# Step 0's bonus as a second run of scores with a second mask, seven weight buffers, step 0's outputs issued from ScalarE's queue, and k's multiplication in other slots

## The chip, the cores and the metric

The kernel runs on one core of a Trainium2 chip. The metric is device time in microseconds (us), a median of runs. TensorE (PE) multiplies matrices, VectorE (DVE), ScalarE (ACT) and GpSimd (POOL) work on tiles, SyncE (SP) issues most of the transfers (DMAs).

## The reference

A recurrent attention over 768 tokens, 4 batches and 8 heads of 48 columns feeds two dense layers:

```python
for t in range(S):
    cur = einsum('bhd,bhe->bhde', u * kt, vt)            # the bonus of the token itself
    y[:, :, t] = einsum('bhd,bhde->bhe', rt, state + cur)
    state = w[..., None] * state + einsum('bhd,bhe->bhde', kt, vt)
x = (sigmoid(x @ w_gate) * (x @ w_val)) @ moe_w_out      # 384 -> 1536 -> 384
out = square(max(x @ w_in, 0)) @ moe2_w_out              # 384 -> 2048 -> 384
```

## The kernel before, in words

**Attention.** The tokens are cut into 6 steps of 128, and a step of one batch is a unit: unit n is step n // 4, batch n % 4. A unit has four inputs: kT and rT (k and r by columns), kv (v and k by rows) and rn (r by rows); lines 98 to 108 load them in the order kv, rn, kT, rT. `attn_prep` (L235) multiplies kT and rT by powers of w on DVE. `attn_scores` (L282) forms all products of r and k on PE. The bonus, r·(u·k) of the same token, is made apart: `attn_pre` (L228) multiplies rn by k and by u on POOL, `attn_sum` (L243) adds up on DVE, and `attn_diag` (L251) puts the eight sums on the antidiagonal of `am` with eight ACT instructions. `attn_mask` (L323) copies the scores under the mask into `am` on DVE. `attn_kh` (L259) multiplies the k rows by `th` on POOL (called kh below), and `attn_sums` (L304) forms the unit's state sums from them on PE. `attn_out` (L340) multiplies `am` with v, reads the state, calls the next unit's scores and sums, copies the sums (`us`) and the output (`ys`) out on ACT, and sends `ys` to `xr` with two DMAs, and four more after a step's last unit (L386 to L392).

**Dense layers.** A tile is 128 columns of a hidden layer for 512 tokens. In the first layer it takes 9 matmuls `pg`, 9 matmuls `pv` and, one tile later, 9 matmuls into `two` and `po`. ACT makes the sigmoid of `pg`, DVE multiplies it with `pv` into `s`, ACT casts it to `gh`, and POOL (in step 0's phase) or DVE makes the rest `gl`.

**Weights.** They come as 64-bit words. `convert` (L124) takes one piece further at each call: ACT and DVE work on the raw piece n (L156, L158), DVE joins piece n-1 (L148, `wt_`), ACT casts piece n-2 (L135) and POOL makes its rest (L136, `wu`). Tile f of the first layer needs pieces 3f (pg), 3f+1 (pv) and 3f+2 (out). `load_raw` keeps NRB = 4 raw buffers.

**Order.** It is written out by hand and each engine runs its list in order. Step 0's four units are done first, alone, with matmuls on an idle tile between them (`warm`). Then phase 0 does tiles 0 to 6 of step 0 while the four units of step 1 are put into its slots by `unit_ops` (L474), eight operations each, kh last of all, just ahead of the next unit's `attn_out`. Phase 1 does step 1's 12 tiles with step 2's units in the slots, and so on. Tiles 7 to 11 of step 0 come after step 5.

**Completion counters.** The program gives its DMAs eight counters in turn, and a DMA is issued only when the one before it on the same counter has landed.

Of the kernel before, what the change touches and what calls it, by code (L numbers as in the profile page):

```python
# [7 lines left out]
F32 = mybir.dt.float32  # L8
# [12 lines left out]
L = 64  # L21
# [21 lines left out]
def tile_kernel(  # L43
# [31 lines left out]
    w_sb = cp.tile([DP, HP], F32, name="w_sb")  # L75
    u_bc = cp.tile([C, H * D], F32, name="u_bc")
# [10 lines left out]
    first = [  # L87
        [wp.tile([P, m], F32, tag="w", name="first", bufs=NW) for _, m, _ in PIECES]
        for _ in range(IN_W)
    ]  # L90
# [73 lines left out]
    def tables():  # L164
# [9 lines left out]
        q = lambda j: px[:, :, j : j + 1].to_broadcast([DP, HP, R])  # L174
        p0 = sp.tile([DP, HP, R], F32, tag="am", name="p0", bufs=2)
        nc.gpsimd.memset(d1, 0.0)
# [91 lines left out]
    def mm64(bank, q, out, lhsT, rhs):  # L270
# [11 lines left out]
    def attn_scores(n):  # L282

        if n >= NU:
            return
        k, r = k_t[n], r_t[n]
        banks, pa_t[n] = (1, 2), pas
        if n < B:

            two = pp.tile([P, 2, T], F32, tag="o", name="pa0")  # L290
            banks, pa_t[n] = (3, 4), two[:, :, 0 : HP * L].rearrange("p r (j t) -> p r j t", j=HP)
            opened.difference_update([(m, q) for m in banks for q in range(2)])
        pa = pa_t[n]
# [46 lines left out]
    def attn_out(n):  # L340
# [18 lines left out]
        if n + 1 < B:  # L359
            attn_scores(n + 1)  # L360
        for j in range(HP):
# [23 lines left out]
        x = xraw[c]  # L385
        nc.sync.dma_start(out=x[0:48, :, b], in_=ys[0:48, b, 0:KT])  # L386
        nc.sync.dma_start(out=x[48:96, :, b], in_=ys[64:112, b, 0:KT])
        if b == B - 1:
            nc.sync.dma_start(out=x[96:128, 0], in_=ys[0:32, :, KT])
            nc.sync.dma_start(out=x[96:112, 1], in_=ys[32:48, :, KT])  # L390
            nc.sync.dma_start(out=x[112:128, 1], in_=ys[64:80, :, KT])
            nc.sync.dma_start(out=x[96:128, 2], in_=ys[80:112, :, KT])  # L392

# [80 lines left out]
    def unit_ops(c, tiles):  # L474
# [4 lines left out]
        if c == 1:  # L479
            slots[0].append(lambda: (attn_pre(B + 1), attn_prep(B + 1)))  # L480
            slots[1].append(lambda: (attn_kh(B + 1), attn_sum(B + 1)))
            slots[2].append(lambda: (attn_diag(B + 1, 0), attn_diag(B + 1, 1)))
        for b in range(B):
# [129 lines left out]
    with tc.manual_schedule():  # L613
# [25 lines left out]
        attn_scores(0)
        attn_sum(0)  # L640
        attn_diag(0, 0)
        attn_diag(0, 1)
# [3 lines left out]
        attn_mask(0)
        attn_sum(1)
        attn_diag(1, 0)
        attn_sums(0)
        attn_us(0)  # L650
        attn_diag(1, 1)
        for n in range(B):
            m = n + 2
            if m < B:
                attn_pre(m)
                attn_kh(m)
                attn_prep(m)
            warm(WARM_OUT[n])
            attn_out(n)
            if m <= B:  # L660
                attn_mask(n + 1)
            if m < B:
                attn_sum(m)
                attn_diag(m, 0)
                attn_diag(m, 1)
# [120 lines left out]
```

## Time and profile before

| what | us |
|---|---|
| median of 3 runs (lowest to highest) | 977.85 (976.94 to 978.19) |
| the profiled execution, its own time | 979.93 |
| its span in the trace | 978.1 |
| PE busy | 947.2 (97%) |
| DVE, ACT, POOL busy | 450.8, 402.9, 132.4 |

The page's map of 40 slices is full for PE from about the sixth slice on; only the first 120 us or so hold slices in which PE is under 9 tenths and the granted clock under full speed. So the rows of this document are taken from there. The profiled execution lies 2.08 us above the median of the runs.

### The profile page before, as it was taken

How to read it: one execution, taken by the hardware profiler on the slowest of the kernel's cores; microseconds unless marked ns; L12 is line 12 of the kernel's file. 1: busy time of each engine (PE TensorE's matmuls, PEld its weight loads, DVE VectorE, ACT ScalarE, POOL GpSimd, SP SyncE). 2: the span in 40 equal slices, each digit the busy share in tenths (PEclk: the TensorE clock that was granted, in tenths of full speed). 3: DMA queues.
4: the chain of work that ended last, by engine and by line, in shares of the span. 5: the costliest groups of instructions: out<-in, count | busy, mean ns of one | idle time of the engine just before them, and what ended most of it. 6: DMA issues, size and time to landing. Idle time of an engine off the chain costs nothing.

```text
span 978.1 us, 16626 instructions
## 1 busy us (share of the span) xinstructions
PE 947.2 (97%) x6898; PEld 757.1 (77%) x6898; DVE 450.8 (46%) x742; ACT 402.9 (41%) x826; POOL 132.4 (14%) x121
## 2 busy tenths in 40 slices
PE   7788899999999999999999999999999999999997
PEld 4466678888888888887888888888888888888886
DVE  5677756754344345423344364433433433434332
ACT  3765565533333323322466463332422322323322
POOL 7455544200000000000133121000000000000000
PEclk7987999999999999999999999999999999999999
DMA  8674545532122222001244540010100100100000
GB/s 305 179 254 140 157 151 153 172 92 64 53 61 85 66 87 88 18 8 44 90 125 127 162 130 1 1 64 1 38 28 1 65 0 1 65 1 1 32 1 33
DMA packets 42235, 76.86 MB, mean 79 GB/s; under 512 B 5168, under 2 KB 17584, under 8 KB 42160
## 3 DMA queue, kind: packets, MB, share of 16 engines
q1 hardware_dynamic: 42160, 75.80, 24.5%
q8 instruction: 54, 0.88, 0.4%
q14 instruction: 21, 0.17, 0.1%
HBM read 60.05 MB, written 11.01 MB: 73 GB/s over the span
## 4 chain that ended last, share of the span: by engine, by line
PE 89%; DVE 2%; DMA 2%; POOL 2%; ACT 1%; SPq 1%; issue 1%; DVEq 0%; POOLq 0%; ACTq 0%
PE pg L445 35%; PE two L464 16%; PE pv L445 15%; PE po L464 12%; PE att L464 7%; PE att L272 4%; DMA first<-in_rkv 2%; SPq L104 1%; DMA xr<-ys 0%; POOL wu L136 0%; POOL gl L428 0%; ACT am L257 0%; ACT raw L156 0%; PE pw L611 0%; POOL first L264 0%
## 5 line engine op out<-in xcount | busy, mean ns | idle before, releaser
L445 PE MATMUL pg<-xh,wu 128*128 128x512 f32 x1008 | 318.3, 400 | 6.5 <-ACT wu L135 3.1
L445 PEld LDWEIGHTS pg<-xh,wu 128*128 128x128 f32 x1008 | 191.0, 190 | 55.6 <-ACT wu L135 3.6
L445 PE MATMUL pg<-xl,wu 128*128 128x512 f32 x504 | 196.7, 398 | 0.3 <-DVE xl L428 0.2
L597 ACT CAST gh<-s 128x512 fp32r<-128x512 f32 (+1 forms) x169 | 104.7, 620 | 192.5 <-DVE s L593 119.0
L596 DVE TENSOR_TENSOR s<-s 128x512 f32<-128x512 f32 (+1 forms) x97 | 66.6, 687 | 181.5 <-ACT s L595 181.5
L428 DVE TENSOR_TENSOR gl<-s,gh 128x512 fp32r<-128x512 f32 x162 | 111.5, 688 | 78.1 <-PE po L464 57.7
L464 PE MATMUL two<-gh,wu 128*128 128x512 f32 x472 | 147.3, 393 | 0.0
L445 PE MATMUL pv<-xh,wu 128*128 128x512 f32 x432 | 141.2, 408 | 1.5 <-POOL wu L136 1.4
L593 DVE TENSOR_TENSOR s<-pv,s 128x512 f32<-128x512 f32 x72 | 49.6, 689 | 197.4 <-PE pv L445 193.8
L595 ACT ACTIVATE s<-pg 128x512 f32<-128x512 f32 (+1 forms) x97 | 57.6, 594 | 190.4 <-PE pg L445 190.4
L445 PEld LDWEIGHTS pg<-xl,wu 128*128 128x128 f32 x504 | 95.9, 190 | 23.7 <-DVE xl L428 1.1
L464 PE MATMUL po<-gh,wu 128*128 128x512 f32 (+1 forms) x338 | 105.4, 392 | 0.0
L464 PEld LDWEIGHTS two<-gh,wu 128*128 128x128 f32 x472 | 88.8, 189 | 21.4
L445 PEld LDWEIGHTS pv<-xh,wu 128*128 128x128 f32 x432 | 81.4, 192 | 22.8 <-POOL wu L136 2.1
L464 PE MATMUL two<-gl,wu 128*128 128x512 f32 x236 | 92.5, 392 | 0.0
L579 ACT ACTIVATE s<-pg 128x512 f32<-128x512 f32 x72 | 43.8, 608 | 112.6 <-PE pg L445 112.5
L445 PE MATMUL pv<-xl,wu 128*128 128x512 f32 x216 | 86.1, 399 | 0.0
L464 PEld LDWEIGHTS po<-gh,wu 128*128 128x128 f32 x338 | 63.4, 188 | 14.8
L156 ACT ACTIVATE raw<-raw 128x384 bf16<-128x384 bf16 x68 | 73.6, 1082 | 0.0
L464 PE MATMUL po<-gl,wu 128*128 128x512 f32 (+1 forms) x169 | 66.2, 392 | 0.0
L464 PE MATMUL att<-gh,wu 128*128 128x512 f32 (+1 forms) x204 | 63.4, 392 | 0.0
L464 PEld LDWEIGHTS two<-gl,wu 128*128 128x128 f32 x236 | 44.2, 187 | 10.0 <-POOL gl L428 0.3
(298 smaller groups left out, 922.5 us busy)
## 6 DMA issues: line engine op xcount, KB each, us to landing
raw<-in_w SPq DMA_DIRECT2D x68, 384.0 KB, 3.1
kv<-in_rkv SPq DMA_DIRECT2D x16, 384.0 KB, 3.6
xin<-x2d SPq DMA_DIRECT2D x6, 768.0 KB, 4.2
out<-x2s SPq DMA_DIRECT2D x18, 256.0 KB, 2.1
first<-in_rkv SPq DMA_DIRECT2D x16, 256.0 KB, 5.5
kT<-in_rkv SPq DMA_DIRECT2D x16, 256.0 KB, 4.6
rT<-in_rkv SPq DMA_DIRECT2D x16, 256.0 KB, 5.0
x2d<-x2s SPq DMA_DIRECT2D x15, 256.0 KB, 2.0
```

The lines of the kernel that those rows point to most:

```text
L104: nc.sync.dma_start(out=got[i][0], in_=got[i][1])
L156: nc.scalar.activation(top, top, AF.Prelu, scale=2.0**-112, alpha=2.0**32)
L272: nc.tensor.matmul(out, lhsT=lhsT, rhs=rhs, start=(bank, q) not in opened, stop=True, skip_group_check=True)
L428: (eng or nc.vector).tensor_tensor(out=dst, in0=src, in1=high.bitcast(F32), op=ALU.subtract)
L445: nc.tensor.matmul(ps, lhsT=a, rhs=b_, start=(i == 0), stop=(i == len(pairs) - 1))
L464: nc.tensor.matmul(po[k][:, ts], lhsT=a, rhs=b_[:, ts], start=(first and m == 0), stop=(last and m == 2 and ts is cuts[-1]),)
L579: nc.scalar.activation(s, pg, AF.Sigmoid)
L593: nc.vector.tensor_tensor(out=s[:, ts], in0=pv[:, ts], in1=s[:, ts], op=ALU.mult)
L595: nc.scalar.activation(s[:, ts], pg[:, ts], AF.Relu)
L596: nc.vector.tensor_mul(s[:, ts], s[:, ts], s[:, ts])
L597: nc.scalar.copy(gh[:, ts], s[:, ts])
```

## The change

For units 0 to 3 the bonus is no longer summed apart. ACT multiplies rT by u·w into a spare tile (`attn_bonus`), PE forms all products a second time with it (`attn_scores0`), into `pas`, and DVE copies them under a second mask, the antidiagonal, into `am`, which POOL has set to zero once. So `attn_pre`, `attn_sum` and `attn_diag` are gone for units 0 to 3, and those units load no rn. Their outputs are issued by ACT. kh moves to the slot of `attn_prep`. There are seven raw buffers, unit 5 and three more raw pieces are loaded at the start, and there are fewer `warm` matmuls.

```diff
-    NRB = 4
+    NRB = 7
-    WARM0, WARM_OUT, WARM_X = 13, (8, 2, 4, 4), (4, 14)
+    WARM0, WARM_OUT, WARM_X = 9, (2, 2, 2, 2), (4, 14)
...
-        for i in (2, 3, 0, 1):
+        for i in (2, 3, 0, 1) if c else (0, 1, 2):
             nc.sync.dma_start(out=got[i][0], in_=got[i][1])
-            if n == 0 and i == 3:
-                nc.sync.dma_start(out=u_bc, in_=u.to_broadcast([C, H * D]))
+            if n == 0 and i == 1:
+                nc.sync.dma_start(out=maskf, in_=mask)
+                nc.sync.dma_start(out=anti, in_=antid)
...
+    def attn_bonus(n):
+        for j in range(HP):
+            nc.scalar.mul(first[n][3][0:DP, j * C : (j + 1) * C], r_t[n][:, j], uw[:, j : j + 1])
...
+    def attn_scores0(n):
+        attn_scores(n)
+        products((1, 2), pas, k_t[n], first[n][3][0:DP, 0:HC].rearrange("p (j t) -> p j t", j=HP))
...
-        m = mask8.unsqueeze(1).unsqueeze(1).to_broadcast([C, 2, HP, L])
-        nc.vector.copy_predicated(am, m, pa_t.pop(n))
+        for m, pa in ((mask8, pa_t.pop(n)),) + (((anti8, pas),) if n < B else ()):
+            nc.vector.copy_predicated(am, m.unsqueeze(1).unsqueeze(1).to_broadcast([C, 2, HP, L]), pa)
...
         if n + 1 < B:
-            attn_scores(n + 1)
+            attn_scores0(n + 1)
+            settle(kv)
...
-        nc.sync.dma_start(out=x[0:48, :, b], in_=ys[0:48, b, 0:KT])
-        nc.sync.dma_start(out=x[48:96, :, b], in_=ys[64:112, b, 0:KT])
+        eng = nc.sync if c else nc.scalar
+        eng.dma_start(out=x[0:48, :, b], in_=ys[0:48, b, 0:KT])
+        eng.dma_start(out=x[48:96, :, b], in_=ys[64:112, b, 0:KT])
...
-                lambda n=n: attn_prep(n + 2),
+                lambda n=n: (attn_kh(n + 2), attn_prep(n + 2)),
...
-                lambda n=n: attn_kh(n + 2),
+                lambda: None,
...
+        load_unit(B + 1)
+        for n in range(4, NRB):
+            load_raw(n)
...
-        load_unit(B + 1)
         attn_pre(B)
```

**ACT, from unit 2's sums to step 0's last output.** In the program before (`us`, `ys`, `raw`, `am` as above; the last two rows are unit 4's diagonal and sums):

```order
L336 COPY us<-att 112x192 x2
L384 COPY ys<-att 112x4x64 x2
L257 ACTIVATE am<-anti,dv 128x64 x8
L156 ACTIVATE raw<-raw 128x384
L336 COPY us<-att 112x192 x2
L384 COPY ys<-att 112x4x64 x2
L156 ACTIVATE raw<-raw 128x384
L384 COPY ys<-att 112x4x64 x2
L257 ACTIVATE am<-anti,dv 128x64 x8
L336 COPY us<-att 112x192 x2
```

In the changed program, from unit 3's sums on:

```order
L363 COPY us<-att 112x192 x2
L412 COPY ys<-att 112x4x64 x2
L416 DMA xr<-ys 48x3x128
L417 DMA xr<-ys 48x3x128
L166 ACTIVATE raw<-raw 128x384
L412 COPY ys<-att 112x4x64 x2
L416 DMA xr<-ys 48x3x128
L417 DMA xr<-ys 48x3x128
L419 DMA xr<-ys 32x4x128
L420 DMA xr<-ys 16x4x128
L421 DMA xr<-ys 16x4x128
L422 DMA xr<-ys 32x4x128
```

One group of eight `am` rows (unit 3's) is gone between unit 2's sums and unit 3's output, and DMA rows stand between the copies.

**The counters that ACT's first outputs wait for.** SP's list in the changed program, with numbers and waits (raw_168 is raw piece 3; first_102, first_103, first_100 and first_101 are unit 5's kv, rn, kT and rT):

```order
L113 DMA first_97<-in_rkv 128x512 [waits DMAHW7_49]
L132 DMA raw_168<-in_w1 128x384 [waits DMAHW0_49]
L113 DMA first_102<-in_rkv 128x768 [waits DMAHW1_49]
L113 DMA first_103<-in_rkv 128x384 [waits DMAHW2_49]
L113 DMA first_100<-in_rkv 128x512 [waits DMAHW3_49]
L113 DMA first_101<-in_rkv 128x512 [waits DMAHW4_49]
```

ACT's list in the changed program, units 0 and 1 (L282 is unit 3's bonus):

```order
L412 COPY ys_379<-att_114 112x4x64 x2
L416 DMA xr_380<-ys_379 48x3x128 [waits DMAHW0_49,Activation_49,Pool_49]
L417 DMA xr_380<-ys_379 48x3x128 [waits DMAHW1_49]
L282 ACTIVATE first_95<-first_93,uw_74 112x128 [waits DMAHW7_49,DVE_49]
L282 ACTIVATE first_95<-first_93,uw_74 112x128 x3
L363 COPY us_478<-att_114 112x192 [waits PE_49]
L363 COPY us_478<-att_114 112x192
```

The outputs of unit 0 follow raw_168 and first_102 on counters 0 and 1, since all loads of the start stand earlier in the program.

**POOL in phase 0, units 6 and 7.** Before (L232 and L233 are the bonus products, L264 is kh, L136 a weight piece's rest, L428 `gl`):

```order
L232 TENSOR_TENSOR first_105<-first_105,first_104 128x384
L233 TENSOR_TENSOR first_105<-first_105,u_bc_73 128x384
L136 TENSOR_TENSOR wu_926<-wt__900,wu_926 128x384
L428 TENSOR_TENSOR gl_917<-s_784,gh_916 128x512
L136 TENSOR_TENSOR wu_949<-wt__929,wu_949 128x384
L136 TENSOR_TENSOR wu_979<-wt__952,wu_979 128x384
L264 TENSOR_TENSOR first_104<-first_104,th_75 128x384
```

In the changed program (L245, L246, L277, L146, L458 in their place):

```order
L245 TENSOR_TENSOR first_107<-first_107,first_106 128x384
L246 TENSOR_TENSOR first_107<-first_107,u_bc_75 128x384
L277 TENSOR_TENSOR first_106<-first_106,th_77 128x384
L146 TENSOR_TENSOR wu_961<-wt__934,wu_961 128x384
L458 TENSOR_TENSOR gl_951<-s_818,gh_950 128x512
```

kh of unit 6 moved from behind three weight pieces and a `gl` to the place ahead of them.

## Rows read from the trace of the kernel before

**Rows 1.** Windows by stage: length; PE, PEld, DVE, ACT, POOL busy; clock; DMA share, GB/s.

```profile
0.00:38.06 38.06, 29.62 (x603) 17.58 (x603) 21.23 (x36) 21.95 (x71) 21.04 (x27) 0.87 0.68 229
38.06:117.81 79.75, 64.33 (x717) 49.56 (x717) 60.42 (x89) 46.68 (x103) 47.62 (x39) 0.85 0.67 209
117.81:131.57 13.76, 11.81 (x162) 8.66 (x163) 6.24 (x14) 6.36 (x19) 2.39 (x3) 0.88 0.30 95
131.57:978.10 846.53, 841.46 (x5418) 681.25 (x5417) 362.94 (x606) 327.92 (x636) 61.36 (x53) 1.00 0.19 59
```

**Rows 2.** Waits of PE, 30 to 140 us: total us, times, longest us.

```profile
PE att L272 <- POOL first L264: 5.8, 2, 3.9
PE pg L445 <- ACT wu L135: 3.1, 1, 3.1
PE att L272 <- POOL kv L264: 2.6, 2, 1.6
...
PE pv L445 <- POOL wu L136: 1.4, 2, 0.9
```

**Rows 3.** Timeline of ACT ahead of phase 0: start, us, instruction, count.

```profile
25.44 0.54 ACT L336 COPY us<-att 112x192 f32<-112x192 f32 x2 [0.29 <-PE att L272]
...
26.45 2.02 ACT L257 ACTIVATE am<-anti,dv 128x64 f32<-128x64 f32 x8
28.37 1.05 ACT L156 ACTIVATE raw<-raw 128x384 bf16<-128x384 bf16 x1
...
37.31 1.73 ACT L432 CAST xh<-xr 128x512 fp32r<-128x512 f32 x3
```

**Rows 4.** Timeline of SP's queue, one of step 0's outputs.

```profile
35.45 0.60 SPq L391 DMA_DIRECT2D xr<-ys  x1
```

**Rows 5.** Timeline of POOL at unit 4's arrival, and its window.

```profile
22.81 1.42 POOL L232 TENSOR_TENSOR first<-first 128x384 f32<-128x384 f32 x1 [0.59 <-DMA first<-in_rkv]
...
20.00:22.00 2.00, 1.89 (x98) 1.71 (x90) 1.62 (x3) 0.00 (x0) 1.92 (x3) 0.96 1.06 392
```

**Rows 6.** Timeline of POOL in phase 0.

```profile
59.70 1.26 POOL L232 TENSOR_TENSOR first<-first 128x384 f32<-128x384 f32 x1 [1.75 <-DMA first<-in_rkv]
...
86.20 1.00 POOL L136 TENSOR_TENSOR wu<-wt__1143,wu 128x384 fp32r<-128x384 f32 x1 [4.59 <-ACT wu L135]
...
88.39 1.31 POOL L264 TENSOR_TENSOR first<-first,th 128x384 f32<-128x384 f32 x1
```

**Rows 7.** Windows over nine matmuls each, columns as in Rows 1.

```profile
91.35:95.30 3.95, 3.95 (x10) 3.14 (x10) 2.64 (x3) 2.47 (x6) 2.14 (x3) 0.51 0.18 44
...
125.56:129.26 3.70, 3.70 (x15) 2.88 (x10) 0.00 (x0) 1.09 (x4) 0.00 (x0) 0.55 0.74 230
...
144.12:146.22 2.10, 2.10 (x14) 1.42 (x16) 1.34 (x3) 2.09 (x3) 1.91 (x2) 1.00 0.59 187
```

**Rows 8.** Timeline of DVE in phase 0.

```profile
42.73 2.43 DVE L241 TENSOR_TENSOR first<-first,trk 112x512 f32<-112x512 f32 x2 [0.73 <-DMA first<-in_rkv]
...
75.72 1.04 DVE L413 TENSOR_TENSOR state<-us,wdec 112x192 f32<-112x192 f32 x1
...
79.98 0.35 DVE L413 TENSOR_TENSOR state<-mid,wdec 112x192 f32<-112x192 f32 x1
```

**Rows 9.** Timeline of ACT and PE around unit 6's output and tile 5.

```profile
84.13 0.62 ACT L597 CAST gh<-s 128x512 fp32r<-128x512 f32 x1 [2.81 <-DVE s L593]
...
91.94 0.66 ACT L384 COPY ys<-att 112x256 f32<-112x256 f32 x2
...
100.42 0.50 PE L445 MATMUL pv<-xh,wu 128*128 128x512 f32 x1 [0.54 <-POOL wu L136]
```

**Rows 10.** Timeline from unit 7's last matmul to phase 1.

```profile
108.68 1.06 PE L445 MATMUL pg<-xh,wu 128*128 128x512 f32 x2
...
116.64 0.62 ACT L432 CAST xh<-xr 128x512 fp32r<-128x512 f32 x1 [5.33 <-DMA xr<-ys]
...
117.81 2.24 PE L445 MATMUL pg<-xh,wu 128*128 128x512 f32 x6 [1.02 <-ACT s L579]
```

More of the change, by code (lines that the diff above doesn't have):

```diff
@@ L74, in tile_kernel @@
     seven = cp.tile([P, 1], F32, name="seven")
-    w_sb = cp.tile([DP, HP], F32, name="w_sb")
+    anti8 = cp.tile([C, L], U8, name="anti8")
+    wu_sb = cp.tile([DP, 2, HP], F32, name="wu_sb")
+    w_sb = wu_sb[:, 0]
+    uw = cp.tile([DP, HP], F32, name="uw")
     u_bc = cp.tile([C, H * D], F32, name="u_bc")
@@ L87, in tile_kernel @@
     first = [
-        [wp.tile([P, m], F32, tag="w", name="first", bufs=NW) for _, m, _ in PIECES]
-        for _ in range(IN_W)
+        [
+            wp.tile([P, HC if n < B and tag == "rn" else m], F32, tag="w", name="first", bufs=NW)
+            for tag, m, _ in PIECES
+        ]
+        for n in range(IN_W)
     ]
@@ L174, in tables @@
         q = lambda j: px[:, :, j : j + 1].to_broadcast([DP, HP, R])
-        p0 = sp.tile([DP, HP, R], F32, tag="am", name="p0", bufs=2)
+        p0 = sp.tile([DP, HP, R], F32, tag="gl", name="p0", bufs=2)
         nc.gpsimd.memset(d1, 0.0)
@@ L187, in tables @@
         nc.vector.tensor_mul(trk[:, :, 0:CENT], p0, q(2))
+        nc.vector.tensor_mul(uw, w_sb, wu_sb[:, 1])
         for i in range(2):
@@ L212, in tile_kernel @@
     am_t, dv_t, pa_t = {}, {}, {}
+    am0 = [sp.tile([C, H, L], F32, tag="am", name="am0", bufs=2) for _ in range(2)]
     bank, us_t, mid_t = {}, {}, {}
@@ L292, in attn_scores, with products @@
             opened.difference_update([(m, q) for m in banks for q in range(2)])
-        pa = pa_t[n]
+        products(banks, pa_t[n], k, r)
+    def products(banks, pa, k, r):
         for j in range(HP):
@@ L325, in attn_mask @@
             return
+        if n < B:
+            am_t[n] = am0[n % 2]
         am = am_t[n].rearrange("p (j r) t -> p r j t", r=2)
-        m = mask8.unsqueeze(1).unsqueeze(1).to_broadcast([C, 2, HP, L])
-        nc.vector.copy_predicated(am, m, pa_t.pop(n))
+        for m, pa in ((mask8, pa_t.pop(n)),) + (((anti8, pas),) if n < B else ()):
+            nc.vector.copy_predicated(am, m.unsqueeze(1).unsqueeze(1).to_broadcast([C, 2, HP, L]), pa)
     def attn_us(n):
@@ L385, in attn_out @@
         x = xraw[c]
-        nc.sync.dma_start(out=x[0:48, :, b], in_=ys[0:48, b, 0:KT])
-        nc.sync.dma_start(out=x[48:96, :, b], in_=ys[64:112, b, 0:KT])
+        eng = nc.sync if c else nc.scalar
+        eng.dma_start(out=x[0:48, :, b], in_=ys[0:48, b, 0:KT])
+        eng.dma_start(out=x[48:96, :, b], in_=ys[64:112, b, 0:KT])
         if b == B - 1:
[L389 to L392, printed above, removed]
+            eng.dma_start(out=x[96:128, 0], in_=ys[0:32, :, KT])
+            eng.dma_start(out=x[96:112, 1], in_=ys[32:48, :, KT])
+            eng.dma_start(out=x[112:128, 1], in_=ys[64:80, :, KT])
+            eng.dma_start(out=x[96:128, 2], in_=ys[80:112, :, KT])
     decay = wdec.unsqueeze(2).to_broadcast([DP, HP, D])
@@ L479, in unit_ops @@
         if c == 1:
-            slots[0].append(lambda: (attn_pre(B + 1), attn_prep(B + 1)))
-            slots[1].append(lambda: (attn_kh(B + 1), attn_sum(B + 1)))
+            slots[0].append(lambda: (attn_pre(B + 1), attn_kh(B + 1), attn_prep(B + 1)))
+            slots[1].append(lambda: attn_sum(B + 1))
             slots[2].append(lambda: (attn_diag(B + 1, 0), attn_diag(B + 1, 1)))
@@ L617, in tile_kernel @@
         nc.scalar.activation(seven, seven, AF.Sigmoid)
-        nc.sync.dma_start(out=w_sb, in_=wt)
+        nc.sync.dma_start(out=wu_sb, in_=wt)
         id_sb = sp.tile([DP, D], F32, tag="ev", name="id_sb", bufs=2)
+        nc.sync.dma_start(out=id_sb, in_=ident)
         maskf = sp.tile([C, L], F32, tag="ev", name="maskf", bufs=2)
-        nc.sync.dma_start(out=id_sb, in_=ident)
         load_unit(0)
-        nc.sync.dma_start(out=anti, in_=antid)
-        nc.sync.dma_start(out=maskf, in_=mask)
         load_unit(1)
@@ L628, in tile_kernel @@
         load_unit(3)
+        nc.sync.dma_start(out=u_bc, in_=u.to_broadcast([C, H * D]))
         load_raw(1)
@@ L632, in tile_kernel @@
         load_raw(3)
+        load_unit(B + 1)
+        for n in range(4, NRB):
+            load_raw(n)
         powers = tables()
-        attn_pre(0)
+        for am in am0:
+            nc.gpsimd.memset(am, 0.0)
         nc.gpsimd.tensor_copy(mask8, maskf)
-        attn_pre(1)
+        nc.gpsimd.tensor_copy(anti8, anti)
         attn_prep(0)
+        attn_bonus(0)
         state_tables(*powers)
[L639 to L642, printed above, removed]
+        attn_scores0(0)
+        attn_mask(0)
         attn_kh(0)
+        attn_sums(0)
         attn_kh(1)
         attn_prep(1)
[L646 to L649, printed above, removed]
+        attn_bonus(1)
         attn_us(0)
-        attn_diag(1, 1)
         for n in range(B):
@@ L654, in tile_kernel @@
             if m < B:
-                attn_pre(m)
                 attn_kh(m)
                 attn_prep(m)
+                attn_bonus(m)
             warm(WARM_OUT[n])
             attn_out(n)
-            if m <= B:
+            if n + 1 < B:
                 attn_mask(n + 1)
[L662 to L665, printed above, removed]
             if n in (1, 2):
                 convert()
-        load_unit(B + 1)
         attn_pre(B)
@@ L738 @@
     kr = np.zeros((NCH, B, P, 2, HP, C), np.float32)
-    wr = np.ones((DP, HP), np.float32)
+    wr = np.ones((DP, 2, HP), np.float32)
     ident = np.zeros((DP, D), np.float32)
@@ L744 @@
             kr[:, :, o : o + D, i] = a[:, :, par::2].transpose(0, 1, 4, 2, 3)
-        wr[o : o + D] = np.asarray(w)[par::2].T
+        for i, a in enumerate((w, u)):
+            wr[o : o + D, i] = np.asarray(a)[par::2].T
         ident[o : o + D] = np.eye(D, dtype=np.float32)
```

## The prediction, made before the changed kernel ran

> **What bounds the kernel now.** First the windows by stage [rows 1]: after 131.57 us PE is busy 841.46 of 846.53 us at the full clock, so nothing that the change does to other engines shows there, and it gives PE no work there. What can change lies in the first 131.6 us: 38.06 us before the first tile, 79.75 us of phase 0 and 13.76 us at phase 1's start. In phase 0 PE is busy 64.33 us at a mean clock of 0.85: 15.4 us are waits, and a part of the busy time is half clock. (Nine matmuls take 2.10 us at full clock [rows 7], and 7 tiles less the last output product are 20 such groups, 42 us; the rest is the attention's small matmuls and the lower clock.)
>
> Then PE's waits from 30 to 140 us [rows 2]: four are for kh (L264), 5.8 + 2.6 = 8.4 us, the longest 3.9 and, in phase 1, 1.6; 3.1 us are for a weight piece of tile 1; 1.4 us for pieces of pv, twice, at most 0.9. Behind two of the kh waits the granted clock is near 0.5, which is the 1.2 GHz level: 3.95 and 3.70 us for nine matmuls where 2.10 is the full clock's [rows 7]. So a long kh wait costs its own length and 1.6 to 1.85 us more.
>
> Last the lists ahead of the first tile. ACT's instructions from unit 2's sums at 25.44 to the first x cast at 37.31 follow each other almost without a pause, 11.87 us [rows 3]. The loads of the start run at 392 GB/s, and unit 4's kv and rn are there at 22.81 us [rows 5].
>
> **The start: a later first tile.** Removed on ACT in that stretch: one group of eight diagonals, 26.45 to 28.37, 1.92 us [rows 3] (the three groups ahead of it and all POOL and DVE work on the bonus go as well, but they end before the point that decides). Added: ten of the twelve output issues of step 0. On SP's queue one takes 0.60 us [rows 4]; on ACT nothing else runs meanwhile, since the next row of ACT's list stands behind it. The trace has no issue on ACT, so I bound it: 0.1 us if most of it lies beside other work, 1.0 if it also drains ACT. I take 0.6, ten are 6.0 us.
>
> When does this stretch begin? Unit 0's output issue waits for the counter of raw piece 3, its second for unit 5's kv. Before unit 4's kv and rn had landed, 6.51 MB were moved (four units of 1.114 MB, three raw pieces of 0.393, u, masks and identity 0.29, kv and rn 0.59). In the new order 6.64 MB end with raw piece 3: 0.13 MB at 392 GB/s is 0.35 us, so 22.8 + 0.3 = 23.1 us, and kv's 0.393 MB are 1.0 us more, 24.1. ACT, which I see at unit 0's output by about 15 us (no sums, no diagonals, kT and rT loaded first), stands until then; behind it stand unit 3's bonus, unit 2's sums and all further outputs, and PE waits for these. Then 0.6 for the issue and four bonus products at some 0.27 (an `am` product of half the width costs 2.02 / 8 = 0.25 [rows 3]), and unit 2's sums start at about 25.8 us, against 25.44. So what the faster bonus wins is lost to this wait. From there 11.87 - 1.92 + 6.0 = 15.95, so the first x cast starts at 41.75, or up to 0.6 earlier if an issue covers one of ACT's short waits for PE, against 37.31. **+4.3 us** (bounds: issue 0.1 gives -0.7, issue 1.0 gives +8.3).
>
> The Trainium skill (DMA: Bandwidth & Descriptors, Issuing engines are not separate DMA queues) says that issuing from several engines saves only the sequencer's time, usually small beside the transfer. Here that time is moved from a queue that computes nothing to one that the first tile waits for; by "small" the term would be the -0.7 above, by the row it is +4.3.
>
> **Phase 0: kh's waits.** Seven raw buffers I cost at nothing: in phase 0 no instruction waits for a raw piece, and a raw load is still released by the same join of pieces. Unit 5's early load takes away 0.73 us of DVE's wait, and its two products, 2.43 us beside POOL [rows 8], could take 1.4. But POOL's three instructions on unit 5 (bonus products, kh) now run just when DVE makes the three rests of x, and such pairs hold each other up: the state product takes 1.04 us beside POOL and 0.35 alone [rows 8], and three such delays of 0.69 would be 2.1. I set the whole to 0, half way (bounds -2.1, that is 0.73 and 1.4, and +2.1).
>
> The Trainium skill (SBUF — State Buffer, SBUF: two separate sides) calls this pair of engines' shared port an exclusive lock for the whole instruction. The two state rows agree; by it alone each of the three rests would wait for a whole POOL instruction, about 1 us, and the term would be near +3.
>
> kh of unit 6 now stands ahead of tile 2's pv piece, on which PE already waits up to 0.9 us [rows 2] because POOL starts unit 6 late, at 59.70, behind its load [rows 6]: +1.0 there. After that kh is ready when PE asks: the waits at units 6, 7 and 8 (1.9, 3.9, 1.0) and the half clock behind the 3.9 (1.85) go, 8.65 us in all, and 1.9 more if the clock also stays up behind unit 6; less the 1.0 that makes 9.5 at most.
>
> What is late next? Unit 7's sums waited for kh at 88.39, behind a piece at 86.20 for which POOL waited 4.59 us on ACT [rows 6]. ACT's list there, from `gh` at 84.13 to unit 6's output, has `gh` 0.6, eight diagonals 2.0, two casts with raw pieces 2.6, a sigmoid 0.6, sums and output 1.0: 6.8 us of work, spread by PE's wait to 92.60 (91.94 + 0.66) [rows 9]. Without the wait it ends at 84.13 + 6.8 = 90.9, and since `gh` hangs on DVE, which the shorter wait at unit 6 brings forward by some 1.5 us, at 89.3: -3.3. From that output a fixed chain follows (mask, four state products, join, `s`, `gh`, cast, rest) to tile 5's pv at 100.42 [rows 9], 7.8 us, so pv starts at 97.1, not 7 us earlier as PE would. PE now waits there some 3 us, which I charge with a lower clock over a part of its nine matmuls (+1.0), and the wait of 1.0 at unit 8 goes. Unit 7's last matmul comes **3.3 us** earlier by this (bounds 0 and -9.5).
>
> From it to phase 1 the chain is again fixed: 108.68 to 117.81, 9.13 us of copies, loads, output DMAs and the x cast, which waited 5.33 us for them [rows 10]. A faster tile 6 doesn't shorten it.
>
> **Phase 1.** The wait of 1.6 us for kh and 1.6 us of half clock behind it [rows 2, 7] lie in a stage where POOL had nothing to do ahead of `gl`; PE has its operands. **-3.2 us** (bounds -3.2, and -1.6 if the clock falls at phase 1's start instead, where PE now waits longer).
>
> **Sum.** +4.3 - 3.3 - 3.2 = -2.2 us. The profiled execution of 979.93 (span 978.1) becomes 977.7; it lay 2.08 above the median, so 977.85 - 2.2 = 975.65, **975.6 us**.
>
> **Rivals.**
> 1. Phase 0 follows PE: the casts come in time, all kh waits and both half clocks go. For it: ACT is busy only 46.68 us of 79.75 there [rows 1]. Against it: the chain above. +4.3 - 9.5 - 3.2 = -8.4: 969.4 us.
> 2. An issue on ACT is nearly free: -0.7 - 3.3 - 3.2 = -7.2: 970.6 us. For it speaks the rule above, against it the 0.60 on SP.
> 3. ScalarE's queue decides (slower): an issue costs 1.0 us, because ACT must end its own copy before it and start afresh after it. Ten are 10 us: +8.3 - 3.3 - 3.2 = +1.8: 979.7; with a half clock over tile 0 that is not made up, 981.5. It decides as soon as an issue costs over 0.83 us.
> 4. No change: phase 0 gives back only 1 us because ACT's list starts later there too: +4.3 - 1 - 3.2 = 0: 977.9 us.
>
> **Chances.** Forecast 0.38 (its own range 973 to 978), rival 1 0.17, rival 2 0.12, rival 3 0.20, rival 4 0.13. A measurement of this kernel tells 0.2%, 2 us, from no change. Below 975.9 lie rivals 1 and 2 and about half of the forecast: 0.48. Above 979.8 lie rival 3's greater part and the forecast's upper tail: 0.25. Between: 0.27. The range takes rivals 1 and 3 in: 968.5 to 982.5.
>
> **What would show it.** Right: on ACT, unit 0's first output issue begins near 23 us after a wait of 5 us or more for a DMA; issues of 0.6 us; first `pg` at 41.5 to 43.5 us; no wait of PE for kh anywhere; a new PE wait of 2 to 4 us at tile 5's pv; phase 1's unit 8 at the full clock. Wrong: first `pg` before 39 (rival 2), tile 5's pv without a wait (rival 1), issues of 1 us (rival 3). If PE has new waits after 131 us, the whole frame is wrong.

## The result, and the profile after

| what | before | after |
|---|---|---|
| median, us (lowest to highest) | 978.02 (976.94 to 980.15) | 985.05 (984.28 to 985.49) |
| profiled execution, its own time | 979.93 | 984.28 |
| its span | 978.1 | 982.4 |

The ratio is 1.0069, 95% interval 1.0049 to 1.0089: slower by 0.7%, where 975.6 and a small gain were forecast, and outside the range of 968.5 to 982.5.

First the windows by stage of the changed kernel, cut where [rows 1] cut the kernel before: up to the first `pg`, up to phase 1's first `pg`, and up to the first `two` matmul of phase 1, which stands at 129.26 us in the trace of before. Columns as in [rows 1].

```profile
0.00:49.05 49.05, 36.59 (x718) 26.09 (x724) 19.08 (x37) 19.21 (x55) 13.42 (x23) 0.65 0.65 217
49.05:125.90 76.85, 61.62 (x716) 45.45 (x716) 60.83 (x89) 46.10 (x103) 47.74 (x40) 0.91 0.62 194
125.90:134.10 8.20, 7.84 (x152) 5.59 (x153) 4.27 (x9) 4.95 (x16) 1.27 (x1) 1.00 0.23 70
134.10:982.40 848.30, 843.94 (x5428) 683.74 (x5426) 365.32 (x610) 328.67 (x638) 63.22 (x53) 1.00 0.19 59
```

The first tile is 10.99 us later (49.05 against 38.06). Up to phase 1 that shrinks to 8.09 (125.90 against 117.81), up to the first `two` matmul of phase 1 to 4.85 (134.11 against 129.26). So what stands behind the first tile went as forecast, -2.9 and -3.24 us against -3.3 and -3.2, and the start went wrong. From that `two` matmul on nothing differs: profiled time less that moment is 850.67 us before and 850.17 after, and lies between 850.2 and 851.1 in all 15 kernels profiled here. That moment is used below as "steady point".

The waits of PE from 41 to 150 us (total, times, longest) hold no wait for kh any more, against 8.4 us of them in [rows 2]; weight pieces have taken the first places.

```profile
PE pv L475 <- ACT wu L145: 4.0, 2, 3.7
PE pg L475 <- ACT wu L145: 3.9, 2, 2.5
PE pg L475 <- ACT xh L462: 3.3, 1, 3.3
PE pv L475 <- POOL wu L146: 3.1, 3, 2.3
```

The timeline of PE shows the forecast wait at tile 5's pv (first fence). The second fence is the window over the nine matmuls behind phase 1's unit 8, now at the full clock: 2.10 us, 3.70 in [rows 7].

```profile
107.68 0.80 PE L475 MATMUL pv<-xh,wu 128*128 128x512 f32 x1 [3.74 <-ACT wu L145]
```

```profile
131.90:134.00 2.10, 2.10 (x14) 1.74 (x10) 0.00 (x0) 1.86 (x7) 0.00 (x0) 1.00 0.54 143
```

**The start.** ACT's timeline from unit 1's sums to the first x cast, which answers to [rows 3] (ACTq rows are DMA issues; in brackets the idle time before a row and what ended it):

```profile
19.41 0.54 ACT L363 COPY us<-att 112x192 f32<-112x192 f32 x2 [5.04 <-PE att L290]
19.83 0.66 ACT L412 COPY ys<-att 112x256 f32<-112x256 f32 x2
25.03 0.71 ACTq L416 DMA_DIRECT2D xr<-ys  x1
25.95 0.61 ACTq L417 DMA_DIRECT2D xr<-ys  x1
26.66 1.27 ACT L282 ACTIVATE first<-first,uw 112x128 f32<-112x128 f32 x4 [6.17 <-DMA first<-in_rkv]
27.85 0.51 ACT L363 COPY us<-att 112x192 f32<-112x192 f32 x2
28.25 0.65 ACT L412 COPY ys<-att 112x256 f32<-112x256 f32 x2
28.93 0.59 ACTq L416 DMA_DIRECT2D xr<-ys  x1
...
34.15 0.54 ACT L363 COPY us<-att 112x192 f32<-112x192 f32 x2 [2.86 <-PE att L290]
...
38.56 0.65 ACT L412 COPY ys<-att 112x256 f32<-112x256 f32 x2 [0.94 <-PE att L290]
...
42.48 0.61 ACTq L422 DMA_DIRECT2D xr<-ys  x1
43.47 2.02 ACT L270 ACTIVATE am<-anti,dv 128x64 f32<-128x64 f32 x8 [4.26 <-DMA xr<-ys]
...
48.31 1.72 ACT L462 CAST xh<-xr 128x512 fp32r<-128x512 f32 x3
```

The issues take 0.59 to 0.71 us each, as forecast from SP's 0.60 [rows 4], and ACT stands with unit 0's first one until 25.03 (forecast 23.1). But look at the brackets on `us` at 34.15 and `ys` at 38.56: ACT waits 2.86 and 0.94 us for PE. The list that was to decide has itself something to wait for. VectorE's timeline of the second mask says what PE waited for:

```profile
20.53 0.73 DVE L355 COPY_PREDICATED am<-anti,att 128x512 f32<-128x512 uint8 x1 [6.82 <-ACT ys L412]
...
28.93 0.72 DVE L355 COPY_PREDICATED am<-anti,att 128x512 f32<-128x512 uint8 x1 [5.05 <-ACT ys L412]
...
35.27 0.72 DVE L355 COPY_PREDICATED am<-anti,att 128x512 f32<-128x512 uint8 x1 [4.73 <-ACT ys L412]
```

Each second mask starts just after an output copy (`ys`) of the unit before, after 4.7 to 6.8 us of waiting, since `pas` shares a PSUM bank (the memory that matmuls write to) with `y2`, from which `ys` is copied, and the program puts the accesses to a bank in order. PE's next second run of scores, and its output product, wait for that mask. So a ring has come up that the kernel before did not have at the start: `ys`, second mask, PE, `us`, `ys`. Its trace already held the same wait in phase 0, where the scores lie in `pas` too (waits of DVE from 38 to 118 us: total, times, longest):

```profile
DVE am L328 <- ACT ys L384: 8.5, 4, 3.6
```

And PE does its part of the ring slowly. Its timeline and windows in the changed kernel come first, then those of the kernel before in the same stage:

```profile
16.53 0.34 PE L290 MATMUL att<-am,first 64*48 64x64 f32 x2 [2.18 <-issue]
...
29.71 1.13 PE L290 MATMUL att<-first 48*64 48x64 f32 x32 [1.13 <-DVE am L355]
...
49.05 1.23 PE L475 MATMUL pg<-xh,wu 128*128 128x512 f32 x2 [3.29 <-ACT xh L462]
```

```profile
21.00:28.00 7.00, 6.29 (x157) 5.14 (x154) 2.89 (x4) 1.34 (x5) 3.59 (x3) 0.50 1.02 380
28.00:35.00 7.00, 5.43 (x145) 4.38 (x138) 1.61 (x3) 2.81 (x9) 0.00 (x0) 0.50 0.20 51
```

```profile
22.59 0.69 PE L272 MATMUL pa<-first 48*64 48x64 f32 x32
```

```profile
22.00:26.00 4.00, 3.87 (x129) 2.66 (x124) 2.18 (x4) 3.54 (x15) 3.33 (x4) 1.00 0.47 157
```

32 score products take 1.13 us where they took 0.69: the granted clock is 0.50 (the 1.2 GHz level) from 10 to 42 us, and was 1.00 from 22 us on before. At 14.4 us PE also stops for 2.18 us with no wait that the profile can name ("issue"). Of ACT's 2.86 and 0.94 us, PE's own waits for the mask in those units (1.13 and 0.98) cover 2.11 at most; the rest is PE's list, which is longer by the second run of scores and runs at half the clock.

### The profile page after: what moved, and what is told of

Same layout as the page of the kernel before. It is cut to its first block, busy times and chain, and to the rows that moved or that the text cites. A ratio compares the mean times of both kernels' runs of the same rounds, so it can differ in the third digit from the quotient of the medians.

```text
span 982.4 us, 16815 instructions
## 1 busy us (share of the span) xinstructions
PE 950.0 (97%) x7012; PEld 760.9 (77%) x7018; DVE 449.5 (46%) x743; ACT 398.9 (41%) x810; POOL 125.6 (13%) x116
## 4 chain that ended last, share of the span: by engine, by line
PE 88%; DVE 4%; ACT 3%; DMA 3%; issue 1%; SPq 1%; ACTq 0%; POOL 0%; DVEq 0%
PE pg L475 34%; PE two L494 16%; PE pv L475 15%; PE po L494 11%; PE att L494 7%; PE att L290 4%; DMA first<-in_rkv 1%; ACT raw L166 1%; ACT am L270 1%; DMA u_bc<-in_u 1%; DVE first L254 1%; DMA xr<-ys 1%; DVE xl L458 0%; DVE am L355 0%; DVE state L443 0%
## 5 line engine op out<-in xcount | busy, mean ns | idle before, releaser
L458 DVE TENSOR_TENSOR gl<-s,gh 128x512 fp32r<-128x512 f32 x162 | 111.5, 688 | 83.2 <-ACT gh L627 54.9
```

Of the source, the lines that this page charges most:

```text
L458: (eng or nc.vector).tensor_tensor(out=dst, in0=src, in1=high.bitcast(F32), op=ALU.subtract)
```

## The experiments

Ratios are to the kernel before, with 95% intervals; differences in us below are those of two ratios times 978.4. "First pg" and the steady point are from each run's trace. A trace is one execution: that of before lies 1.9 us above its median, that of e2_sp_out 3.3, those of e1_warm and e3_own_bank 1.6 and e7_kh_early 1.2, and that of e5_old_bonus lies 1.6 below. So prices are taken from the medians, and traces only show what waits for what.

| run | median, us | ratio | first pg | steady point |
|---|---|---|---|---|
| before | 978.02 | 1 | 38.06 | 129.26 |
| changed kernel | 985.05 | 1.0069 [1.0049, 1.0089] | 49.05 | 134.11 |
| e1_warm | 983.88 | 1.0054 [1.0035, 1.0073] | 48.70 | 134.79 |
| e2_sp_out | 980.92 | 1.0033 [1.0019, 1.0047] | 46.45 | 133.42 |
| e3_own_bank | 982.77 | 1.0048 [1.0034, 1.0062] | 45.80 | 134.20 |
| e4_kh_only | 974.85 | 0.9970 [0.9957, 0.9983] | 39.38 | 123.46 |
| e5_old_bonus | 983.36 | 1.0048 [1.0036, 1.0060] | 44.91 | 131.25 |
| e6_own_sp | 979.34 | 1.0004 [0.9991, 1.0017] | 43.48 | 129.87 |
| e7_kh_early | 978.40 | 1.0005 [0.9991, 1.0018] | 40.12 | 128.95 |
| e8_own_sp_warm | 976.98 | 0.9985 [0.9974, 0.9995] | 41.40 | 125.49 |
| e9_own_late | 976.68 | 0.9980 [0.9968, 0.9993] | 38.72 | 126.21 |
| e10_own_quiet | 976.21 | 0.9980 [0.9967, 0.9992] | 40.68 | 125.38 |
| e11_after_late | 985.53 | 1.0080 [1.0067, 1.0093] | 50.20 | 134.86 |
| e12_own_spread | 976.96 | 0.9986 [0.9970, 1.0002] | 41.13 | 124.23 |
| e13_unit4_first | 975.30 | 0.9964 [0.9951, 0.9978] | 40.30 | 126.21 |

**Old idle-tile matmuls in the changed kernel.**

```diff
-    WARM0, WARM_OUT, WARM_X = 9, (2, 2, 2, 2), (4, 14)
+    WARM0, WARM_OUT, WARM_X = 13, (8, 2, 4, 4), (4, 14)
```

> The changed kernel with the idle-tile matmuls of the kernel before: 13 at the start and 8, 2, 4, 4 ahead of the units, instead of 9 and 2, 2, 2, 2. Theory A, clock: the granted clock was 0.50 from 10 to 42 us in the changed kernel and 1.00 from 22 us on before, and half clock is what stretches units 1 to 3; the extra matmuls lift it, PE's part of units 2 and 3 falls from 5.2 us to about 3, the first pg comes at 45 us instead of 49.05, and the whole takes about 981 instead of 985. Theory B, ring (second mask waits for the output copy of the unit before): PE still stands idle in each unit, the clock falls back, and ten more matmuls lie in the chain: first pg at 49 to 52 us, 985 to 988.

-1.5 us, with overlapping intervals; the first pg moved by 0.35. The windows show the granted clock (third number from the right), PE's row the stop between them:

```profile
10.00:17.00 7.00, 4.62 (x145) 3.18 (x147) 4.03 (x6) 2.88 (x10) 2.68 (x3) 1.00 0.96 352
...
18.00:19.00 1.00, 1.00 (x21) 0.44 (x13) 0.00 (x0) 0.47 (x3) 0.00 (x0) 0.90 1.02 406
...
21.00:28.00 7.00, 5.60 (x116) 3.95 (x108) 1.29 (x3) 2.24 (x8) 2.96 (x3) 0.50 1.02 379
```

```profile
16.64 0.38 PE L290 MATMUL att<-am,first 64*64 64x64 f32 x11 [1.65 <-issue]
```

The clock was full until close to 19 us and then fell. What lies ahead of the fall is not a wait for the ring (PE's first wait for the second mask behind unit 0 is 0.28 us at 20.43, after the fall) but a stop of 1.65 us that the profile can't name. Idle-tile matmuls alone do not hold the clock; the first pg is near theory B's 49 to 52, but its reason is not shown.

**Outputs from SyncE again.**

```diff
-        eng = nc.sync if c else nc.scalar
+        eng = nc.sync
```

> The changed kernel with step 0's outputs issued by SyncE's queue again. Theory C, ScalarE's queue: the wait for a completion counter (1.25 us of it count, since unit 2's sums were ready at 26.6 and copied at 27.85) and the six issues behind unit 3's output (3.9 us) go: about -5 us, 980; the four issues of units 1 and 2 lie beside PE's work and give nothing. By the prediction's own sum all ten count, 6.1 and 1.9 us, -8: 977. By theories A and B alone the ring sets the pace and at most 1 us goes: 984 to 985.

-3.5 us (0.36%), nearer to theory C's 5 than to the prediction's own 8. The ring stayed (in a trace 3.3 us above the median): `us` of units 2 and 3 at 26.89 and 33.95, 7 us apart. PE's timeline and a window:

```profile
26.77 1.03 PE L641 MATMUL pw<-idle 128*128 128x512 bf16 x2
27.73 1.14 PE L290 MATMUL pa<-first 48*64 48x64 f32 x32
```

```profile
21.00:28.00 7.00, 6.88 (x162) 5.39 (x162) 4.19 (x4) 2.43 (x10) 3.73 (x3) 1.00 1.02 373
```

The clock column reads 1.00, yet 32 products take 1.14 us and two idle-tile matmuls 1.03, against 0.69 and 0.60 at 22 us in the kernel before, and 1.13 for the products at the granted 0.50 of the changed kernel: by its durations the work ran as at half clock, and they are what to go by. The traces of e6_own_sp and e11_after_late show the same.

**Second run of scores in PSUM banks of its own.**

The second mask is then copied in two halves, and the idle-tile matmuls write to another bank; only the products are shown.

```diff
...
-        products((1, 2), pas, k_t[n], first[n][3][0:DP, 0:HC].rearrange("p (j t) -> p j t", j=HP))
+        own = [pp.tile([P, T], F32, tag=tag, name="pb0") for tag in ("o2", "g")]
+        pb_t[n] = [t[:, 0 : HP * L].rearrange("p (j t) -> p j t", j=HP) for t in own]
...
+        products((5, 6), pb_t[n], k_t[n], first[n][3][0:DP, 0:HC].rearrange("p (j t) -> p j t", j=HP))
```

> The changed kernel with the second run of scores in two PSUM banks of its own, so that its mask no longer waits for the output copy of the unit before; the mask is copied in two halves. Theory B: three times ScalarE's copies (1.05 us) and the mask (0.73) leave the ring, -4 to -6 us, 979 to 981, first pg at 43 to 45 us; if PE then stands idle so little that the clock rises, up to 2 us more. Theory A or C alone: 0 to -1 us, 984 to 985.

-2.1 us with overlapping intervals, the first pg 3.25 earlier; beside SyncE's queue (below) the same edit gives 2.8 us with intervals apart. So the ring has a price, less than expected. No second mask waits for `ys` any more (where it waits in this trace, it is for PE's products). The time of one unit fell to 4.75 us (`us` at 27.23 and 31.98), but this is not the pace of a unit without the ring, since PE had run ahead while ACT stood at unit 0's output issue until 24.44; beside SyncE's queue it is 6.81 (below). And PE stopped in unit 1:

```profile
21.66 1.09 PE L290 MATMUL att<-am,first 64*64 64x64 f32 x29 [3.50 <-issue]
```

**The new slot of kh alone, in the kernel before**.

```diff
...
-                lambda n=n: attn_prep(n + 2),
+                lambda n=n: (attn_kh(n + 2), attn_prep(n + 2)),
...
-                lambda n=n: attn_kh(n + 2),
+                lambda: None,
```

> The kernel before with only the new slot of k's multiplication. The two traces put the gain behind the first tile at 2.9 us up to phase 1 and 3.35 in phase 1. If the new slot makes it: -6.2 us against the kernel before, 971.8, with no wait of PE for that product left. Rival: the gain in phase 0 came from the 11 us later start, by which loads and weight pieces were further ahead; then only the 3.3 us of phase 1 remain, 974.7. Third: the waits move to weight pieces, 977 to 978.

-2.9 us by the ratio, near the 3.3 of the first rival. Yet the pair of traces gives -5.8 at the steady point, with the first pg 1.3 later (x waited 1.31 us for an output), so 7.1 us behind the first tile. The two agree when one sees that the execution of before that was profiled lay 1.5 to 2 us above its median, this one 0.8 below. That suggests that a part of the waits in [rows 2] was that execution's own; no second trace of before shows it.

**The changed kernel without its bonus**: the kernel before with the new slot, the early loads of the next diff, and outputs from ScalarE.

```diff
...
+        eng = nc.sync if c else nc.scalar
...
-        nc.sync.dma_start(out=x[0:48, :, b], in_=ys[0:48, b, 0:KT])
+        eng.dma_start(out=x[0:48, :, b], in_=ys[0:48, b, 0:KT])
...
```

> The changed kernel without its bonus: sums on GpSimd and VectorE, diagonals on ScalarE and the idle-tile matmuls of the kernel before, with seven buffers, early loads, outputs from ScalarE and the new slot. Theory C, ScalarE's queue is the price: here ScalarE's list ahead of the first tile is full, so each of the ten issues counts: 6.1 us and a counter wait of 1 to 4 us, first pg at 45 to 48 us, 978.3 - 3.4 + 7 = 982. Theory B with A, the second run of scores (the ring, the half clock) is the price: the issues fit beside PE's work, first pg at 39 to 41 us, 975 to 977.

**The same with outputs from SyncE** (new slot and early loads only).

```diff
-    NRB = 4
+    NRB = 7
...
         load_raw(3)
+        load_unit(B + 1)
+        for n in range(4, NRB):
+            load_raw(n)
...
-        load_unit(B + 1)
         attn_pre(B)
```

> The kernel before with the new slot, seven buffers and unit 5 and three pieces loaded at the start (outputs from SyncE, old bonus). The prediction set these loads at 0 (-2.1 to +2.1): then 974.9, as with the new slot alone. If SyncE's queue is now held at a counter of the last early piece, unit 0's output is issued later but long before the first tile needs it: 0. Rival: the loads bring GpSimd's work on unit 5 beside VectorE's first rests: +2, 977.

These two differ by ScalarE's queue alone: 1.0005 against 1.0048, **4.2 us**, first pg 40.12 against 44.91. Theory C holds. In the first of them unit 0's output is issued right behind its copy (22.06 us), so this price contains no counter wait like the changed kernel's. There PE waits ahead of the first tile for ScalarE's cast:

```profile
44.91 3.11 PE L446 MATMUL pg<-xh,wu 128*128 128x512 f32 x6 [5.45 <-ACT xh L433]
```

The Trainium skill (DMA: Bandwidth & Descriptors, Issuing engines are not separate DMA queues) calls the time that an issue takes on its sequencer usually small relative to the DMA itself. The changed kernel's trace agrees: 0.59 to 0.71 us for an issue on ScalarE, 2.3 to 3.7 us from issue to landing. But small beside its transfer is not small on an engine whose list the first tile waits for: the twelve issues cost 4.2 us in all.

And against the new slot alone the early loads cost 3.4 us by the medians, which the prediction had at 0. Between the two traces the steady point is 5.49 us later; 0.74 us of that lie ahead of the first tile, where PE stops in unit 3's scores:

```profile
27.31 0.63 PE L272 MATMUL pa<-first 48*64 48x64 f32 x28 [1.49 <-issue]
```

The rest lies behind, in the same matmuls at a lower clock. From the first tile to the steady point PE is busy 72.55 us for 869 matmuls here (first row) and 67.97 us for 868 with the new slot alone (second row), at a mean clock of 0.87 and 0.92, and idle about 16 us in both:

```profile
40.12:128.95 88.83, 72.55 (x869) 53.95 (x869) 65.30 (x97) 51.40 (x118) 48.77 (x41) 0.87 0.57 178
```

```profile
39.38:123.46 84.08, 67.97 (x868) 51.26 (x869) 64.72 (x97) 50.87 (x118) 48.39 (x41) 0.92 0.64 200
```

Why the clock is lower there these runs do not settle.

**Banks of its own and SyncE's queue together (the diffs of e3 and e2); the same with the old idle-tile matmuls (that of e1).**

> The changed kernel with both edits that won alone: the second run of scores in PSUM banks of its own (-2.0 alone) and step 0's outputs from SyncE's queue (-3.5 alone). If the two prices are separate they add up: 985.05 - 5.5 = 979.5. If each hid the other (with one gone the chain followed the other), the gain is more: 976 to 978, first pg at 41 to 43 us. If the half clock of units 1 to 3 sets the pace, 980 to 982, with 32 products at 1.1 us throughout.

> As the run with both edits, and with the idle-tile matmuls of the kernel before (8 ahead of unit 0, then 2, 4, 4). Theory A: with no ring and no long wait the clock lifted by the 8 matmuls holds; 32 products take 0.65 to 0.7 us instead of 1.1 in units 1 to 3, a unit's PE work falls from 5.2 to 3 us, and the first pg comes 3 to 5 us earlier than without them: about 3 us less in time. Rival: PE stops for another reason in unit 1 (the stops of 1.3 to 3.5 us that no wait explains, each beside a transfer of PE's instructions), the clock falls again, and the time is that of the run without them, +1 to +2 for the added matmuls.

Together -6.4 us from the changed kernel; the single gains add up to 5.6, so the two prices nearly add up. With both gone a unit still takes 6.81 us (`us` at 25.42 and 32.23), 3.3 to 3.7 in the kernel before:

```profile
32.23 0.54 ACT L369 COPY us<-att 112x192 f32<-112x192 f32 x2 [4.76 <-PE att L290]
```

From 13 us to unit 3's output at 35.89 PE has no wait over 0.7 us in that trace, and 32 products take 1.1 us throughout. So without the ring it is PE's own list, with the second run of scores at the durations of half clock, that sets the pace.

The idle-tile matmuls, which alone gave nothing sure, give 1.9 more now (intervals just overlap), less than hoped: the trace of the last one has two stops of PE, in a stretch in which the DMA engines are full (last column but one of the window).

```profile
14.81 0.38 PE L290 MATMUL att<-am,first 64*48 64x64 f32 x11 [1.85 <-issue]
...
21.54 0.37 PE L290 MATMUL pb<-first 48*64 48x64 f32 x3 [3.28 <-issue]
```

```profile
17.00:21.00 4.00, 1.14 (x59) 1.00 (x59) 1.43 (x3) 2.01 (x8) 1.00 (x1) 0.99 1.03 394
```

**The loads of the kernel before: with all three edits, and in the changed kernel alone** (e7's diff backwards).

> The run with PSUM banks of its own, outputs from SyncE and the old idle-tile matmuls, now with the loads of the kernel before too: four raw buffers, unit 5 and the later pieces not at the start. With the new slot alone the early loads had cost 3.5 us (974.85 against 978.4). If that price stands by itself: 977.0 - 3.5 = 973.5. If it came only from one stop of PE that the longer full stretch of the DMA engines made (unit 3, 1.5 us) and its half clock, it shows here only where PE stops after 23 us; the stops at 13 and 18 us stay: 976 to 977.

> The changed kernel with the loads of the kernel before alone (four raw buffers, unit 5 loaded behind step 0). Theory C: unit 0's output on ScalarE no longer waits for raw piece 3's counter and its neighbours; unit 2's sums are copied at 26.6 instead of 27.85 and 1.3 us go: 983.7. If the early loads cost 3.5 us here too: 981.5. Prediction's own account (raw buffers 0, unit 5's load 0): 985.

No gain in either (0.9980 against 0.9985; 1.0080 against 1.0069). The price of the early loads is not a fixed one. In the changed kernel unit 0's output was now issued at 21.16 us instead of 25.03, but `us` of unit 2 came only 0.65 us earlier, since ACT then waited for PE. And ScalarE's queue found another counter to wait for, among the last outputs, 2.9 us between these rows:

```profile
39.51 0.61 ACTq L420 DMA_DIRECT2D xr<-ys  x1
43.02 0.59 ACTq L421 DMA_DIRECT2D xr<-ys  x1
```

**Quiet DMA engines while units 1 and 2 run.** To the edits of e9 (banks of its own, SyncE's queue, old idle-tile matmuls, old loads) comes a later issue: in e10 four weight pieces, u and unit 4 all stand behind unit 0's output; in e12 in three portions, as in the diff; in e13 `load_unit(4)` and the line of `load_raw(1)` and u change places.

```diff
...
             attn_out(n)
+            if n == 0:
+                load_raw(0)
+                load_raw(1)
+            if n == 1:
+                nc.sync.dma_start(out=u_bc, in_=u.to_broadcast([C, H * D]))
+                load_unit(4)
+            if n == 2:
+                load_raw(2)
+                load_raw(3)
...
```

> As the run with the old loads, and in addition the first four weight pieces, unit 4 and u are issued only behind unit 0's output, so that the DMA engines are idle from about 12 to 17 us, where two transfers of PE's instructions fall. Theory D, the stops of 1.85 and 3.28 us are PE waiting for its instructions behind the bulk loads: both go, the clock then holds, unit 3's sums are copied at 26 to 28 us instead of 31.85 and the first pg comes at 36 to 38 us instead of 41.4: 969 to 971. Rival: the stops have another cause; they stay, the later loads make the first tile wait for its pieces, and the time is 975 to 978.

> As the run with the quiet DMA stretch, but the bulk loads in three portions: two weight pieces behind unit 0's output, u and unit 4 behind unit 1's, two pieces behind unit 2's, so that no stretch of full DMA engines lasts over 4 us. There PE had stopped 4.92 us in unit 2's output (25.6 to 30.6 us), inside the stretch of bulk loads, while unit 3's sums stood ready at 24.72. Theory D: no stop over 1.5 us is left, the clock holds, unit 3's output comes at 27 to 29 us instead of 33.08 and the first pg at 35 to 38 us instead of 40.7; 970 to 973 if the weight pieces keep up. Rival: the stop stays near 25 us although the engines are not full there: 976.

> As the run with three portions, but unit 4 and one piece behind unit 0's output, u and a piece behind unit 1's, two pieces behind unit 2's. There unit 4's columns landed at 32.9 us and PE waited 5.3 us for them, which ate what the missing stops had won (unit 3's output at 28.34, first pg only at 41.13). If that load was all that held the first tile: no such wait, first pg at 36 to 38 us, 971 to 974, the second run of scores being no slower than the old bonus. Rival 1: unit 4's larger portion falls on the transfer of PE's instructions near 20 us, PE stops 2 us or more, first pg at 39 to 41, 976 to 977. Rival 2: the first tile comes early but waits as much longer for its weight pieces: 976.

The long stops move with the bulk loads. The one in unit 1 was 3.28 us in e8 and 1.63 in e9 (first row below); with everything behind unit 0's output it is 0.25, and a new one of 4.92 us comes where the bulk loads now lie (second fence, of e10):

```profile
20.95 0.28 PE L290 MATMUL pb<-first 48*64 48x64 f32 x3 [1.63 <-issue]
```

```profile
18.19 0.28 PE L290 MATMUL pb<-first 48*64 48x64 f32 x3 [0.25 <-issue]
...
30.56 1.12 PE L290 MATMUL att<-am,first 64*64 64x64 f32 x32 [4.92 <-issue]
```

```profile
17.00:21.00 4.00, 3.60 (x155) 2.90 (x149) 1.50 (x3) 2.21 (x9) 0.06 (x1) 1.00 0.29 54
24.00:31.00 7.00, 2.03 (x52) 1.40 (x48) 1.58 (x4) 2.14 (x5) 0.25 (x1) 0.77 1.00 339
```

In three portions no stop over 0.54 us is left and unit 3's output is copied at 28.34 us (31.94 in the kernel before), but PE waits 5.29 us for unit 4's columns:

```profile
18.77 0.28 PE L290 MATMUL pb<-first 48*64 48x64 f32 x3 [0.54 <-issue]
...
34.54 1.14 PE L290 MATMUL att<-first 48*64 48x64 f32 x32 [5.29 <-DVE first L254]
```

With unit 4 first that wait is gone, and stops of 1.72 and 2.18 us are back (rival 1). What these stops are: in these traces the instruction queue moves single packets of 16 KB, about 3.5 to 8.6 us apart. In every trace with a stop over 1.2 us one of them starts at most 1.3 us ahead of the stop or within it (in e10 at 28.2, 2.6 us after the stop of 4.92 began). That PE waits for its own instructions behind the bulk loads fits that, and the moved stop. It is a reading: no run takes that transfer away, and full DMA engines with such a packet are not enough. In e2 and e6 the DMA share is 1.02 to 1.05 from 17 to 28 us, packets start there at 20.5 and 27.0 and at 19.0 and 25.5, and no such stop is over 0.54 us.

The last of these, 0.9964, and the new slot alone, 0.9970, are the fastest here. Their intervals overlap, so even in its best arrangement the second run of scores shows no gain over the old bonus.

## Why the prediction was wrong

| part | predicted, us | measured, us |
|---|---|---|
| kh's slot (phase 0 and 1) | -6.5 | -2.9 (e4) |
| raw buffers, unit 5's load | 0 | +3.4 (e7 over e4) |
| issues on ScalarE | +6.0 (ten) | +4.2 (all twelve, e5 over e7) |
| the rest of the start: bonus by PE | -1.7 | +2.1 (changed over e5; intervals overlap) |
| sum | -2.2 | +6.8 |

The rows hold for this order of adding the parts: taken out of the changed kernel alone, the early loads give nothing (e11). The rest of the start also holds the counter wait at unit 0's output and the fewer idle-tile matmuls.

The traces tell nearly the same. Between the two profiled executions the time rose by 4.35 us where -2.2 was forecast: 6.55 too low, and the start alone (11.0 for 4.3) makes 6.7. Between the medians it rose by 6.8. The further 2.4 us are the two executions, that of before above its median and that of the changed kernel 0.8 below; in the table they would stand in kh's line, by the two readings of e4. The other three lines, 9.7 for 4.3, are the start, with what the early loads cost behind it.

**The step that failed is the start's.** "From there 11.87 - 1.92 + 6.0 = 15.95" takes ACT's list as nearly unbroken, with PE in time for it. In the trace that stretch is 20.46 us (27.85 to 48.31), and it holds 3.80 us of ACT's waits for PE, where the same stretch of the kernel before held 0.65: that is 3.15 of the 4.5 us too many. I had counted what the second run takes off ACT and not what it adds to PE and VectorE: the second mask waits for `ys`, PE for the mask, ACT for PE. The mask covers at most 2.11 of the 3.80 us, and banks of its own give back 2.1 us (not sure) to 2.8; the rest is PE's own longer list at half clock, which e6 shows as the pace once the ring is gone. The first tile came 11.0 us later, not 4.3. Two further parts of the same step: unit 2's sums at 27.85, not 25.8, with unit 0's issue at 25.03, not 23.1 (the loads ran at 350 GB/s from 10 to 17 us, not 392; that this is all of it is not shown). And fewer idle-tile matmuls, of which the prediction says nothing, while the clock stayed at half until 42 us; put back alone they gave nothing sure (e1).

**Price of an issue**: right in the row (0.6), too high in the sum: ScalarE's list was not unbroken even with the old bonus (without the issues, in e7, it waited 2.05 and 1.28 us for PE), so some issues fill waits. Rival 3 (ScalarE's queue decides) named the right sign for a wrong reason: it asked for over 0.83 us an issue.

**Phase 0 and 1**: mechanism and size right in the trace (-2.9, -3.24, the 3.74 us wait at tile 5's pv, no kh wait), but e4 gives half of it in the median. The gain was read from the waits of one execution that lay 2 us above its median, and only the total was corrected for that.

**Early loads**: the zero stood on an argument about raw pieces and on the POOL pair. Beside the old bonus the cost was 3.4 us, outside its bounds of 2.1, and lay in a stop of PE and in its lower clock; in the changed kernel and with all three edits no cost shows. Why the two differ stays open.

## What to carry to other kernels

Work taken off the engine that seems to decide must be followed to the end on the engines that get it: which buffer or bank does it share, whose copy frees that, and does a ring close over one unit. How many matmuls does the receiving engine get, and at which clock does it run there? A gain read off the waits of one execution holds for that execution; where the median lies lower, a part of the waits may be its own. Bulk loads that nobody waits for yet can still cost: 3.4 us in one setting here, nothing in two others.

## What the runs showed of the hardware

- PE stops without a named wait. Those over 2 us (2.18 in the changed kernel, 3.50 in e3, 3.28 in e8, 4.92 in e10, 2.18 in e13) lay where the DMA share was 0.94 to 1.05, and moved with the bulk loads; shorter ones of 1.33 to 1.72 us (e10, e1, e13) also came at shares of 0.47 to 0.77, and in e2 and e6 shares of 1.02 to 1.05 brought none over 0.54.
- The granted clock can read 1.00 over a stretch in which matmuls take 1.65 times as long as at full speed elsewhere (1.14 against 0.69 us for 32 products, in e2).
- A DMA issued by ScalarE holds its list for 0.59 to 0.71 us in the changed kernel (once 1.12 in e5), and for as long as its completion counter is not free: 4.5 us at unit 0's output, 2.9 in the run with the old loads (e11).
